# Putting the second dense layer of seven token tiles into the steps of a recurrence

## The chip, the cores and the metric

The kernel runs on one core of a Trainium2 chip. The metric is the device time of one execution in microseconds (us), the median of several runs. PE is TensorE, DVE VectorE, ACT ScalarE, POOL GpSimd and SP SyncE, which issues most of the DMAs.

## What is computed

Two branches over one sequence of 2048 tokens of width 512, mixed by a gate per token:

```python
g = _sigmoid((x * gate_w).sum(-1, keepdims=True))
a = _A_ref(x, A_mem0, A_Wq, A_Wk, A_Wv, A_Wo, A_seg_len)
b = _B_ref(x, B_w1, B_b1, B_w2, B_b2)
return g * a + (1 - g) * b
```

Branch B is an MLP: layer norm, a first dense layer from 512 to 1376 with a gelu, and a second one back to 512.

Branch A is a recurrence over 64 segments of 32 tokens. In each, 8 memory rows are put ahead of the segment's 32 tokens; the 40 rows go through attention with 32 heads of 128 and an output projection; and the first 8 rows of the result are the next segment's memory:

```python
for s in range(n_seg):
    h = jnp.concatenate([mem, xs], axis=1)
    q = jnp.einsum('btd,dhe->bhte', h, Wq)
    ...
    o = jnp.einsum('bhte,hed->btd', o, Wo)
    mem = o[:, :M, :].copy()
    outs.append(o[:, M:, :])
```

## The kernel before

All is written for one core in an order that the author fixes by hand (`manual_schedule`): each engine takes its instructions in the order in which the program emits them, and the framework only adds the waits. Line numbers are those of the kernel before, as the profile has them.

**The MLP comes first.** Tokens stand in 16 tiles of 128; a block is two tiles, so there are eight blocks (0 to 7). A block has 11 chunks of 128 hidden columns. A unit is one chunk of one block: `a_mm` (L458) computes the first layer of both tiles in four matmuls of 256 columns (L462) into one of two PSUM banks, SbF and W in turn, and ACT's gelu (L463) writes the chunk to `hTm`, of which there are two for blocks in turn. Two units later `b_mm` (L465) adds the chunk's part of the second layer, one matmul of 512 columns per tile (L468), in a bank per tile (`bp`, U[0] to U[3]). After the last chunk `ct_out` (L480) multiplies by 1 - g and stores the tile to a DRAM buffer, `c_dr`. In chunk 0 DVE takes the gates of the block before (`gates`, L449, after a tanh on ACT) and prepares the next block's layer norm (`prep`, L416); at chunks 6 and 7 (7 and 8 in block 0) PE transposes its two tiles (`prep_tr`, L437) and DVE then sums the gates (`gate_sums`, L444). The constants for the mask (L391 to L394) are made on DVE at chunk 9. At chunk 8 `loads` (L341) issues input tiles and the recurrence's weights on SP. Block 7 has the first projections of the recurrence beside it (`first`, L498: 24 units of four matmuls).

**The recurrence has 64 steps**, four (si = 0 to 3) to a token tile T. Memory rows and 24 of the tokens form the 32 columns `hT`; the eight tokens left over of each segment are gathered for a whole tile and projected as side work. PE multiplies in groups of four matmuls that use 32 columns each, side by side (`tile_position`). A step does, in PE's order: queries and keys in four banks, U[0] to U[3] (L122), each cast by ACT (L127) and transposed by DVE (L131); scores (L259, L263) in two halves, in SbF and W, on a mask that DVE has put there (`mask_put`, L250); values in X1 and X2 (L141), with ACT's casts (L719); sums over the memory queries (`msum`, L704: L270 and L273) in U[0] and U[1]; DVE's normalisation (`mnorm`, L707); sums for the token queries (`xsums`, L612: L616); the product with the values in all four U (`av`, L276: L283 and L288); the output projection of the memory rows in W (`wo_pass`, L645: L153); and the transposition that brings the new memory back into `hT` (`new_mem`, L653: L659, DVE's copy L661). After `av` ACT copies the memory part of the four U banks (L746) and then the token part (`x_raw`, L619: L622, four copies, U[3] last); `recip_x` (L625) sends the token part's reciprocals through DRAM back to all partitions (`Rb`), and POOL multiplies in the next step (`x_norm`, L638).

**Side work** is a generator (`side`, L590) that gives one group of PE work at a time; `run(n)` takes n of them at fixed places, W1 before `xsums`, W2 before `wo_pass`, W3 after it, one after each of the first two `new_mem`, and the rest at the end:

```python
WS = ((2, 3, 0), (2, 2, 2), (2, 2, 2), (2, 2, 2))
```

At si = 0 and 1 it is the next tile's left-over queries (X1) and keys (X2), at si = 3 its values (X1, X2), at si = 2 the output projection of the left-over tokens of the tile before (X1). The last tile has none at si = 0 and 1. At si = 0 the output of tile T - 2 is put together (`out_sel`, L221); it reads `c_dr` back (`c_load`, L203).

Of the kernel before, what the change touches and what calls it, by code (L numbers as in the profile page):

```python
# [27 lines left out]
def kernel(ctx, tc, A_x, A_mem0, A_Wq, A_Wk, A_Wv, A_Wo, A_seg_len, B_x, B_w1, B_b1, B_w2, B_b2, gate_w, out):  # L28
# [34 lines left out]
    g_all = pers.tile([P, NT], FP32)  # L63
    c_dr = dram.tile([S, Dm], BF16, name="c_dr")
    r_dr = [dram.tile([P, NG], FP32, name=f"r_dr{i}") for i in range(2)]
# [20 lines left out]
    make_identity(nc, ident[:])  # L86
    nc.gpsimd.memset(b1r[:], 0.0)
# [23 lines left out]
    Sb = [bk[:, 0:4 * EW].rearrange("p (i c) -> p i c", c=EW) for bk in (SbF, W)]  # L111
# [109 lines left out]
    def out_sel(T, bk):  # L221
        for si in range(SPT):
            nc.tensor.matmul(bk[32 * si:32 * si + 32, :], lhsT=SelR[:], rhs=ws.pop(SPT * T + si)[:], start=True, stop=False,
                             skip_group_check=True, tile_position=(0, 32 * si))
        wl = wls.pop(T)
        for si in range(SPT):
            nc.tensor.matmul(bk[32 * si:32 * si + 32, :], lhsT=SelL[:, 32 * si:32 * si + 32], rhs=wl[:], start=False, stop=True,
                             skip_group_check=True, tile_position=(0, 32 * si))

        def ev():  # L230
            o = cw.tile([P, Dm], BF16, tag="o", name="o")
# [15 lines left out]
    RP = [bk[:, 288:320] for bk in (SbF, W)]  # L247


    def mask_put(i2):  # L250
        c = 4 * EW + (NG + 2 * M if i2 == 0 else 0)
        nc.vector.tensor_copy(out=(SbF, W)[i2][:, 0:c], in_=MkF[:, 0:c])
# [41 lines left out]
    with tc.tile_pool(name="mlpw", bufs=1) as mlpw, \  # L294
# [7 lines left out]
        w2_sb = mlpw.tile([P, FC, Dm], BF16)  # L302
# [36 lines left out]
        m0 = ep.tile([M, Dm], BF16)  # L339
# [58 lines left out]
        for i in range(2):  # L398
            nc.gpsimd.memset(hTm[i][FR:FR + 1, FC - 1, :], 1.0)
        z_all = mlpw.tile([P, NT], FP32)  # L400
        omg = mlpw.tile([P, NT], FP32)
# [63 lines left out]
        def b_mm(blk, fc):  # L465
            rows = min(P, F - fc * P + 1)
            for tt in range(TB):
                nc.tensor.matmul(bp(blk, tt)[:], lhsT=hTm[blk % 2][:rows, fc, tt * P:(tt + 1) * P],  # L468
                                 rhs=w2_sb[:rows, fc, :], start=(fc == 0), stop=(fc == FC - 1))
            if fc == FC - 1:  # L470
                if blk < NBLK - 1:
                    ct_out(blk, 0)
                    late.append(lambda: ct_out(blk, 1))
                else:
                    for tt in range(TB):
                        ct_out(blk, tt)

# [39 lines left out]
        for n, (blk, fc) in enumerate(units):  # L517
# [15 lines left out]
            if blk + 1 < NBLK:  # L533
                f0 = 7 if blk == 0 else 6
# [10 lines left out]
            elif fc >= 1:  # L545
                if fc == 1:
                    side0 = first()
# [6 lines left out]
        for n in range(len(units) - LAG, len(units)):  # L554
            b_mm(*units[n])
        for _ in side0:
# [33 lines left out]
    def side(T, si):  # L590
# [14 lines left out]

    XRs, Rbs = {}, {}
# [38 lines left out]
    def wo_pass(U_, cuts=(0, Dm)):  # L645
        for n in range(NW):
            wo_group(W, U_, n)
        w = cw.tile([P, Dm], BF16, tag="w", bufs=8, name="w")
        for a, b in zip(cuts, cuts[1:]):
            nc.scalar.copy(out=w[:, a:b], in_=W[:, a:b])  # L650
# [14 lines left out]
    for s in range(nseg):  # L665
# [38 lines left out]
        def msum(i2):  # L704
            sums(U[i2][:, 320:352].rearrange("p (i q) -> p i q", q=8), E[:, 4 * i2:4 * i2 + 4, :], 40, 48, 8, True)

        def mnorm(i2):  # L707
            r, e = RP[i2], E[:, 4 * i2:4 * i2 + 4, 40:56].rearrange("p i (a q) -> p i a q", q=8)
            nc.vector.reciprocal(out=r, in_=U[i2][:, 320:352])
# [23 lines left out]
        if not last:  # L733
            msum(1)
# [6 lines left out]
        run(W1)  # L741
        xsums(E, 1)
# [7 lines left out]
        w = wo_pass(UT[s % 2], (0, P, 2 * P, Dm))  # L750
# [62 lines left out]
    o = cw.tile([P, Dm], BF16, tag="o", name="o")  # L813
# [128 lines left out]
```

## Time and profile before

| | |
|---|---|
| time, median of 3 runs | 770.31 us (770.07 to 771.1) |
| span of the profiled execution | 768.4 us |
| around that span, in the runs' median | 1.9 us |
| first matmul of the recurrence | 96.06 us after the span's start |

The span runs from the first to the last instruction of one execution that the profiler recorded; the profile gives no other time for it, so the runs' median is set beside it. A timeline row gives start and length in us, engine, line and operation, out<-in with partitions x elements, the count of equal instructions merged, and in brackets the engine's idle time before and what ended it.

### The profile page before, as it was taken

The numbers are of one execution on the slowest core, as the hardware profiler recorded it, in microseconds if no ns is written. First come the engines' busy times: TensorE is split into PE (matmuls) and PEld (weight loads), VectorE is DVE, ScalarE is ACT, GpSimd is POOL, SyncE is SP. The second block draws the span as 40 slices with busy tenths as digits, with TensorE's granted clock in tenths as the row PEclk, the third lists the DMA queues.
The fourth block names the chain that finished last, engine by engine and source line by source line (L and its number), as shares of the span: only waits on it lengthen the run. The fifth ranks groups of instructions, "written<-read, shape, count | busy, mean of one in ns | idle before, by whom it ended". The sixth has DMA issues, their size and how long they took to land.

```text
span 768.4 us, 43822 instructions
## 1 busy us (share of the span) xinstructions
PE 753.4 (98%) x19186; PEld 412.2 (54%) x19186; DVE 396.1 (52%) x1428; ACT 540.0 (70%) x1631; POOL 278.2 (36%) x522
## 2 busy tenths in 40 slices
PE   7999999999999999999999999999999999999996
PEld 5666554555555555555555555555555555555553
DVE  5776355445445454545554554545454555444444
ACT  4666676777777777777777777777777777777763
POOL 4111033433344443334434334443424443343341
PEclk9999999999999999999999999999999999999999
DMA  6779422223222222212131322122222213122221
GB/s 196 274 233 400 153 58 63 76 63 87 65 59 66 79 72 73 80 53 74 58 89 62 90 63 79 45 80 73 80 72 59 76 49 89 62 83 64 72 67 38
DMA packets 53319, 70.58 MB, mean 92 GB/s; under 512 B 21306, under 2 KB 43043, under 8 KB 51587
## 3 DMA queue, kind: packets, MB, share of 16 engines
q1 hardware_dynamic: 51394, 64.84, 26.8%
q8 instruction: 152, 2.49, 1.4%
q0 software_dynamic: 784, 1.97, 0.8%
q10 hardware_dynamic: 944, 0.92, 0.3%
q14 instruction: 45, 0.36, 0.2%
HBM read 56.96 MB, written 4.45 MB: 80 GB/s over the span
## 4 chain that ended last, share of the span: by engine, by line
PE 96%; DMA 1%; DVE 1%; ACT 1%; issue 0%; SPq 0%; POOL 0%; DVEq 0%; ACTq 0%
PE U L122 30%; PE X L141 18%; PE W L153 15%; PE X L122 7%; PE U L468 4%; PE U L283 4%; PE X L153 4%; PE W L462 2%; PE SbF L462 2%; PE U L270 1%; PE W L259 1%; DMA w_sb<-in_B_w_dram 1%; PE U L659 1%; PE SbF L259 1%; PE SbF L616 1%; PE U L288 1%
## 5 line engine op out<-in xcount | busy, mean ns | idle before, releaser
L643 POOL TENSOR_TENSOR UT<-XR,Rb 128x384 bf16<-128x384 bf16 x126 | 140.3, 1136 | 301.7 <-DMA Rb<-r_dr 220.5
L127 ACT CAST Tb<-U 128x512 bf16<-128x512 f32 x258 | 151.2, 586 | 78.4 <-PE U L122 78.1
L122 PEld LDWEIGHTS <-hT 128*32 128x32 bf16 x4096 | 104.5, 96 | 103.9 <-DVE hT L661 8.6
L141 PE MATMUL X<-Wv_sb,hT 128*32 128x512 bf16 x2048 | 143.8, 378 | 0.0
L122 PE MATMUL U<-Wq_sb,hT 128*32 128x512 bf16 x2048 | 136.1, 381 | 0.3 <-DVE hT L661 0.2
L122 PE MATMUL U<-Wk_sb,hT 128*32 128x512 bf16 x2048 | 132.7, 379 | 0.0
L153 PE MATMUL W<-Wo_sb,UT 128*32 128x512 bf16 x2080 | 124.6, 380 | 1.2 <-POOL racc L635 1.2
L661 DVE CAST hT<-U 128x8 bf16<-128x8 f32 x126 | 20.9, 167 | 172.8 <-PE U L659 163.6
L719 ACT CAST V<-X 128x256 bf16<-128x256 f32 x256 | 88.7, 372 | 14.5 <-PE X L141 0.8
L131 DVE STREAM_TRANSPOSE QT<-Tb 128x256 f32<-128x256 f32 x128 | 57.0, 446 | 76.5 <-ACT Tb L127 76.5
L153 PEld LDWEIGHTS <-UT 128*32 128x32 bf16 x2080 | 57.8, 96 | 56.5 <-issue 13.1
L650 ACT CAST w<-W 128x128 bf16<-128x128 f32 (+1 forms) x192 | 46.0, 311 | 48.2 <-PE W L153 48.2
L622 ACT CAST XR<-U 128x256 bf16<-128x256 f32 x252 | 78.4, 434 | 0.0
L131 DVE STREAM_TRANSPOSE KT<-Tb 128x256 f32<-128x256 f32 x128 | 57.0, 445 | 28.0 <-ACT Tb L127 23.5
L643 POOL TENSOR_TENSOR UL<-XR,Rb 128x128 bf16<-128x128 bf16 x126 | 60.3, 502 | 0.0
L141 PEld LDWEIGHTS <-hT 128*32 128x32 bf16 x2048 | 46.4, 94 | 21.0
L635 POOL TENSOR_TENSOR racc<-racc,R 128x72 f32<-128x72 f32 x63 | 21.3, 338 | 93.4 <-PE U L288 84.1
L468 PE MATMUL U<-w_sb,hTm 128*128 128x512 bf16 (+1 forms) x176 | 52.4, 381 | 0.0
L746 ACT CAST UT<-U 128x64 bf16<-128x64 f32 x252 | 35.4, 226 | 22.9 <-PE U L288 22.8
L462 PEld LDWEIGHTS <-w_sb 128*128 128x128 bf16 (+1 forms) x352 | 34.5, 102 | 20.1 <-issue 1.3
L702 ACT ACTIVATE E<-W 128x64 bf16<-128x64 f32 (+1 forms) x128 | 35.0, 273 | 11.3 <-PE W L263 11.3
L659 PEld LDWEIGHTS <-w 128*32 128x32 bf16 x1008 | 22.8, 93 | 37.2 <-ACT w L650 29.3
(159 smaller groups left out, 1204.7 us busy)
## 6 DMA issues: line engine op xcount, KB each, us to landing
Rb<-r_dr SPq DMA_DIRECT2D x63, 512.0 KB, 3.8
Wv_sb<-in_A_Wv_dram SPq DMA_DIRECT2D x4, 1024.0 KB, 6.3
Wq_sb<-in_A_Wq_dram SPq DMA_DIRECT2D x4, 1024.0 KB, 7.1
Wk_sb<-in_A_Wk_dram SPq DMA_DIRECT2D x4, 1024.0 KB, 9.4
Wo_sb<-in_A_Wo_dram SPq DMA_DIRECT2D x4, 1024.0 KB, 15.0
VP<-VL SPq DMA_DIRECT2D x64, 64.0 KB, 3.5
c<-c_dr SPq DMA_DIRECT2D x16, 128.0 KB, 3.6
xt<-in_A_x_dram SPq DMA_DIRECT2D x15, 128.0 KB, 3.1
```

Of the source, the lines that this page charges most:

```text
L122: nc.tensor.matmul(bk[32 * j:32 * j + 32, :], lhsT=G[:, kc, :], rhs=W5[t][:, kc, h0:h1, j, :], start=(kc == 0), stop=(kc == KC - 1), tile_ ...
L127: nc.scalar.copy(out=Tb[:], in_=bk.rearrange("p (a b e) -> p a e b", a=8, b=2))
L131: nc.vector.transpose(out=dst[:, 8 * hf:8 * hf + 8, c0:c0 + 32, :].rearrange("p a r b -> p a (r b)").bitcast(FP32), in_=Tb[:].rearrange("p ...
L141: nc.tensor.matmul(bk[32 * j:32 * j + 32, :], lhsT=G[:, kc, :], rhs=Wv5[:, kc, 4 * vb:4 * vb + 4, j, :], start=(kc == 0), stop=(kc == KC - ...
L153: nc.tensor.matmul(bk[32 * c:32 * c + 32, :], lhsT=U_[:, j, i, :], rhs=Wo_sb[:, 4 * i + j, :], start=(n == 0), stop=(n == NW - 1), tile_po ...
L462: nc.tensor.matmul(hp[:rows, 0:TB * P], lhsT=w1_sb[:, kc, fc * P:fc * P + rows], rhs=yTs[blk][:, kc, :], start=(kc == 0), stop=(kc == KC - 1))
L468: nc.tensor.matmul(bp(blk, tt)[:], lhsT=hTm[blk % 2][:rows, fc, tt * P:(tt + 1) * P], rhs=w2_sb[:rows, fc, :], start=(fc == 0), stop=(fc = ...
L622: nc.scalar.copy(out=XR[:, j], in_=U[j][:, 0:NG * 40].rearrange("p (i q) -> p i q", q=40)[:, :, 0:32])
L643: nc.gpsimd.tensor_tensor(out=out[:, :, 4 * h:4 * h + 4, o:o + b - a], in0=XR[:, :, 4 * h:4 * h + 4, a:b], in1=Rb[:, h, :, :, a:b], op=ALU ...
L650: nc.scalar.copy(out=w[:, a:b], in_=W[:, a:b])
L719: nc.scalar.copy(out=V[:, i0:i0 + 2, :].rearrange("p i e -> p (i e)"), in_=(X1, X2)[vb][:, 256 * h:256 * h + 256])
L746: nc.scalar.copy(out=UT[s % 2][:, j, :, 0:M], in_=U[j][:, 0:NG * 40].rearrange("p (i q) -> p i q", q=40)[:, :, 32:40])
```

## The change

Seven tiles (3, 5, 7, 11, 13, 14, 15) get only the first layer in the MLP. Their activations are stored to DRAM (`spill`) and loaded back chunk by chunk in the recurrence, where the second layer is done in half groups: four matmuls of 32 columns and 256 output columns side by side, two half groups to a chunk. They are taken from a generator, one ahead of `msum(1)` and one after `run(W1)` in each step, and as side work of the last tile at si = 0 and 1. They add up in bank W until a tile's 11 chunks are through, and DVE then scales and stores it. W's other uses move: the second half of the scores to U[0], `wo_pass` to X2, `msum` to U[1] and U[3], the first two `new_mem` to U[0] and U[1], the second stream of the left-over projections from X2 to U[3], and the reciprocals RP[1] to SBUF. In blocks whose second tile is put off, the transposes for the next block are emitted at chunks 8 and 9. Output tiles have one buffer in place of two.

```diff
+    DEF = (3, 5, 7, 11, 13, 14, 15)
+    h_dr = {T: dram.tile([FC, P, P], BF16, name=f"h_dr{T}") for T in DEF}
...
-    Sb = [bk[:, 0:4 * EW].rearrange("p (i c) -> p i c", c=EW) for bk in (SbF, W)]
+    Sb = [bk[:, 0:4 * EW].rearrange("p (i c) -> p i c", c=EW) for bk in (SbF, U[0])]
...
-    RP = [bk[:, 288:320] for bk in (SbF, W)]
+    RS = ep.tile([P, 32], FP32)
+    RP = [SbF[:, 288:320], RS[:]]
...
-            for tt in range(TB):
+            tts = [tt for tt in range(TB) if blk * TB + tt not in DEF]
+            for tt in tts:
                 nc.tensor.matmul(bp(blk, tt)[:], lhsT=hTm[blk % 2][:rows, fc, tt * P:(tt + 1) * P],
...
+        def spill(blk, a, b):
+            for tt in range(TB):
+                T = blk * TB + tt
+                if T in DEF:
+                    src = hTm[blk % 2][:, :, tt * P:(tt + 1) * P]
+                    nc.sync.dma_start(h_dr[T][a:b].rearrange("f p t -> p f t"), src[:, a:b])
...
-                f0 = 7 if blk == 0 else 6
+                f0 = 8 if (blk + 1) * TB - 1 in DEF else 7 if blk == 0 else 6
+                if fc == 2 and blk >= 1:
+                    spill(blk - 1, 0, FC)
...
+                if fc == 2:
+                    spill(blk - 1, 0, FC)
+                if fc == 7:
+                    spill(blk, 0, 6)
...
+        spill(NBLK - 1, 6, FC)
...
-            gens = [[left_qk(T + 1, 0, 0, X1), left_qk(T + 1, 1, 0, X2)], [left_qk(T + 1, 0, 1, X1), left_qk(T + 1, 1, 1, X2)], [],
-                    [left_v(T + 1, 0, X1), left_v(T + 1, 1, X2)]][si]
+            gens = [[left_qk(T + 1, 0, 0, X1), left_qk(T + 1, 1, 0, U[3])], [left_qk(T + 1, 0, 1, X1), left_qk(T + 1, 1, 1, U[3])], [],
+                    [left_v(T + 1, 0, X1), left_v(T + 1, 1, U[3])]][si]
+        elif si < 2:
+            gens = [mlp_units(8)]
...
+    def hm_load(n):
+        for _ in range(n):
+            if work:
+                T, fc = work.pop(0)
+                hm = cw.tile([P, P], BF16, tag="hm", bufs=5, name="hm")
+                nc.sync.dma_start(hm[:], h_dr[T][fc])
+                hms.append((T, fc, hm))
+
+    def mlp_out(T):
+        ct = cw.tile([P, Dm], BF16, tag="o", bufs=1, name="ct")
+        nc.vector.tensor_scalar(out=ct[:], in0=W[:], scalar1=omg[:, T:T + 1], scalar2=None, op0=ALU.mult)
+        nc.sync.dma_start(c_dr[T * P:(T + 1) * P, :], ct[:])
+
+    def mlp_halves():
+        hm_load(4)
+        while hms:
+            T, fc, hm = hms.pop(0)
+            for h in range(2):
+                cc = slice(256 * h, 256 * h + 256)
+                for c in range(4):
+                    nc.tensor.matmul(W[32 * c:32 * c + 32, cc], lhsT=hm[:, 32 * c:32 * c + 32], rhs=w2_sb[:, fc, cc],
+                                     start=(fc == 0 and h == 0), stop=(fc == FC - 1), skip_group_check=True, tile_position=(0, 32 * c))
+                if h == 1:
+                    hm_load(1)
+                    if fc == FC - 1:
+                        mlp_out(T)
+                yield
+
+    def mlp_units(n):
+        for _ in range(n):
+            next(mlp, None)
+            next(mlp, None)
+            yield
...
-        bk = (U[1][:, 0:M], U[3][:, 0:M], xs8z)[n]
+        bk = (U[0][:, 0:M], U[1][:, 0:M], xs8z)[n]
...
-            sums(U[i2][:, 320:352].rearrange("p (i q) -> p i q", q=8), E[:, 4 * i2:4 * i2 + 4, :], 40, 48, 8, True)
+            sums(U[1 + 2 * i2][:, 320:352].rearrange("p (i q) -> p i q", q=8), E[:, 4 * i2:4 * i2 + 4, :], 40, 48, 8, True)
...
         if not last:
+            next(mlp, None)
             msum(1)
             mnorm(1)
...
         run(W1)
+        next(mlp, None)
         xsums(E, 1)
...
-        w = wo_pass(UT[s % 2], (0, P, 2 * P, Dm))
+        w = wo_pass(UT[s % 2], (0, P, 2 * P, Dm), X2)
```

More of the change, by code (lines that the diff above doesn't have):

```diff
@@ L470, in b_mm @@
             if fc == FC - 1:
[L471 to L475, printed above, removed]
-                        ct_out(blk, tt)
+                for tt in tts:
+                    if tt == 0 or blk == NBLK - 1:
+                        ct_out(blk, tt)
+                    else:
+                        late.append(lambda: ct_out(blk, 1))
+        def spill(blk, a, b):
[4 more added lines that the diff above has]
+                    nc.sync.dma_start(h_dr[T][a:b].rearrange("f p t -> p f t"), src[:, a:b])
         late = []
@@ L604, in extra @@
         return iter(())
+    work = [(T, fc) for T in DEF for fc in range(FC)]
+    hms = []
+    def hm_load(n):
[28 more added lines that the diff above has]
+            yield
+    mlp = mlp_halves()
     XRs, Rbs = {}, {}
```

23 lines of the change are left out of this document (12 added, 11 removed).

## The prediction

> **What bounds the kernel now.** I read the cores view first, then parts 1 and 4 of the page.
>
> ```profile
> core 0: 768.4 us, clock 0.996
> PE 753.4 (98%) x19186; PEld 412.2 (54%) x19186; DVE 396.1 (52%) x1428; ACT 540.0 (70%) x1631; POOL 278.2 (36%) x522
> PE 96%; DMA 1%; DVE 1%; ACT 1%; issue 0%; SPq 0%; POOL 0%; DVEq 0%; ACTq 0%
> ```
>
> The reader is to see that the chain that ended last is PE's for 96% of the span. Matmul rows include a pipelined tail, so "busy" doesn't say whether PE has room; starts do. Next, the timeline of one MLP block (PE, then DVE), and of block 7 (PE, then ACT).
>
> ```profile
> 28.88 0.60 PE L462 MATMUL SbF<-yT,w_sb 128*128 128x256 bf16 x4
> 29.32 0.59 PE L468 MATMUL U<-w_sb,hTm 128*128 128x512 bf16 x2
> 29.75 0.60 PE L462 MATMUL W<-yT,w_sb 128*128 128x256 bf16 x4
> ...
> 34.98 0.40 PE L441 MATMUL X<-ident,y 128*128 128x128 bf16 x4
> 35.21 0.60 PE L462 MATMUL W<-yT,w_sb 128*128 128x256 bf16 x4
> ```
> ```profile
> 30.18 0.17 DVE L452 TENSOR_SCALAR g_all<-th 128x2 f32<-128x2 f32 x1 [1.31 <-ACT th L451]
> ...
> 34.51 0.73 DVE L434 TENSOR_SCALAR y<-xt,mv,rs 128x512 bf16<-128x512 bf16 x2
> ...
> 36.51 0.42 DVE L442 COPY yT<-X 128x512 bf16<-128x512 bf16 x1 [0.67 <-PE X L441]
> ...
> 38.67 0.23 DVE L394 TENSOR_SCALAR MkF<-MkF,mk 128x8 bf16<-128x8 bf16 x1
> ```
> ```profile
> 84.03 0.60 PE L462 MATMUL SbF<-yT,w_sb 128*128 128x256 bf16 x4
> ```
> ```profile
> 84.72 0.47 ACT L463 ACTIVATE hTm<-SbF,b_sb 128x256 bf16<-128x256 f32 x1
> ```
>
> One unit there is 0.44 us for L462 plus 0.43 us for two L468, with no gap: PE bounds the MLP, at 0.217 us per second-layer matmul. Four transposes take 35.21 - 34.98 = 0.23. Then a step of the recurrence (24, first of its tile, si = 0) on PE, DVE and ACT.
>
> ```profile
> 344.19 1.11 PE L122 MATMUL U<-Wq_sb,hT 128*32 128x512 bf16 x16
> ...
> 349.57 0.61 PE L141 MATMUL X<-Wv_sb,hT 128*32 128x512 bf16 x8
> 350.08 0.20 PE L270 MATMUL U<-E,BO 128*32 128x32 bf16 x4
> ...
> 350.77 0.22 PE L616 MATMUL SbF<-BO,E 128*32 128x4 bf16 x8
> 350.93 0.30 PE L283 MATMUL U<-E,V 32*128 32x40 bf16 x16
> ...
> 351.21 0.29 PE L283 MATMUL U<-E,V 32*128 32x40 bf16 x16
> ...
> 351.91 0.39 PE L122 MATMUL X<-Wk_sb,GL 128*32 128x512 bf16 x4
> 352.12 1.90 PE L153 MATMUL W<-Wo_sb,UT 128*32 128x512 bf16 x32
> ```
> ```profile
> 350.93 0.22 DVE L710 TENSOR_TENSOR E<-E,W 128x64 bf16<-128x64 bf16 x1
> ```
> ```profile
> 351.57 0.56 ACT L746 CAST UT<-U 128x64 bf16<-128x64 f32 x4 [0.35 <-PE U L288]
> 351.99 1.25 ACT L622 CAST XR<-U 128x256 bf16<-128x256 f32 x4
> ```
>
> A group of four 32-column matmuls runs side by side: 351.91 to 352.12 is 0.216 us for 512 columns, so a half group of 256 takes 0.108. Last, from the chain of waits, two starts of an ordinary si = 1 step, and from the timeline the same step of the last tile, which has no side work.
>
> ```profile
> 355.32 3.45 PE U L122 x63
> 365.46 3.55 PE U L122 x64
> ```
> ```profile
> 728.07 1.05 PE L122 MATMUL U<-Wq_sb,hT 128*32 128x512 bf16 x16
> ...
> 735.41 1.91 PE L153 MATMUL W<-Wo_sb,UT 128*32 128x512 bf16 x32 [0.39 <-POOL racc L635]
> ...
> 738.22 0.62 PE L122 MATMUL U<-Wq_sb,hT 128*32 128x512 bf16 x8
> ```
>
> With eight side units (8 x 0.216 = 1.73 us) the step takes 365.46 - 355.32 = 10.14 us, without them 738.22 - 728.07 = 10.15. So a step is a chain through all engines, side work lies in its gaps, and what delays a link of the chain is paid in full.
>
> **The change part by part.** *Removed.* Seven tiles x 11 chunks = 77 matmuls of L468, 77 x 0.217 = **16.7 us** of PE in the MLP, of which not all comes out:
> - DVE is late next. From the gates (30.18) it needs 5.06 us to both y (35.24), some 4.7 to the first. Then follow on PE that tile's transposes (0.23), one unit with one tile put off (0.44 + 0.22) and the second transposes (0.23), so the second yT copy starts no sooner than some 6.1 us after the gates (4.7 + 1.1, and an estimated 0.2 from PE's last start to DVE's). From that copy to the end of the mask constants DVE needs 38.90 - 36.51 = 2.4. The next gates thus come no sooner than 8.5 us after the last, where PE would be through in 11 x 0.65 + 2 x 0.23 = 7.6. Blocks 1 to 3 hand this on; followed through to block 5's start I lose 2.9 us. Without mask constants, block 6 loses 0.5.
> - Block 7 loses both tiles. Its first-layer units alternate between two banks, and a bank comes free 84.72 + 0.47 - 84.03 = 1.16 us after its matmuls start: 0.58 a unit, not 0.44. Gate tanhs that wait for DVE's sums stand in the same ACT queue. The 24 side units spare half of this; I take 1.0.
>
> That leaves 16.7 - 2.9 - 0.5 - 1.0 = **12.3 us gained** (bounds 9 and 16.7). ACT's and POOL's share of the result copies and stores goes too, off the chain.
>
> *Spills.* A tile's activations leave in 11 x 128 rows of 256 bytes, on SP behind 2 MB of weights. A buffer's gelu two blocks on waits until the spill has read it.
>
> ```profile
> Wq_sb<-in_A_Wq_dram SPq DMA_DIRECT2D x4, 1024.0 KB, 7.1
> VP<-VL SPq DMA_DIRECT2D x64, 64.0 KB, 3.5
> r_dr<-R SPq DMA_DIRECT2D x63, 4.0 KB, 1.5
> ```
> ```profile
> 96.73 1.17 SPq L487 DMA_DIRECT2D c_dr<-ct  x2
> ```
>
> Weights land 7.1 us after issue, a spill behind them some 2 later, and the buffer is wanted about 8.6 us after that issue: 0 to 1.3 us late, for three blocks. I take **1.0 us** (0 to 4).
>
> *First load.* The first activations come back only after the last spills have landed, since their buffers lie where the MLP's lay. From the recurrence's start: last gelu 0.7 us, two issues 1.17, landing 1.5 to 3.5 (r_dr and VP), the load 0.5 to issue and 1.5 to 3.5 to land: 5.4 to 9.4 us. The first half group stands ahead of L270, 350.08 - 344.19 = 5.9 us into a step. I take **1.5 us** once (0 to 4). What waits behind that load on PE is msum(1) and the whole chain.
>
> The Trainium skill ("DMA: Bandwidth & Descriptors", Specifications) says that transfers under 512 B are read, modified and written. No row here shows the spill; r_dr's 32-byte rows landing in 1.5 us against 3.5 for VP's 512-byte rows don't show such a penalty. If the rule doubled the spills' time, the third rival would be the likelier.
>
> *Half groups.* 124 of 154 come two to a step, 0.108 us each. The first fills PE's wait for the exponentials: V's two groups end at 349.57 + 0.43 = 350.00 and L270 starts at 350.08. The second delays L616 and the first L283, but the second L283 (351.21) waits for DVE's E (350.93 + 0.22 = 351.15), and between 350.77 and 351.21 PE has about 0.1 us to give. I take 0.01 us a step, **0.6 us** (0 to 13.4, all of 124 x 0.108 if the gaps weren't there). The seven 512-wide DVE copies, once in eleven steps, stand ahead of the x part's reciprocals; the next step's Wo is the first to need those, and POOL's product is the cover. Cost 0.
>
> *Bank moves.* Scores' second half in U[0], sums in U[1] and U[3], Wo in X2, new memory in U[0] and U[1]: each is read by something that its next writer awaits anyway (U[0]'s next writer needs hT from the same DVE copy). Cost 0; that chain is the cover. One move has none. At si = 0, W2 = 3 puts the first K unit of the next tile between x_raw and wo_pass. It went to X2, free since the V copies; it goes to **U[3]**, which x_raw copies last. In the built program its first matmul waits for ACT's count after the fourth L622. PE works in order: Wo's eight groups, the memory rows and the next step are queued behind it. The same pair of rows in the first and in the last of the 15 steps that have it (T = 0 to 14):
>
> ```profile
> 103.39 0.39 PE L122 MATMUL X<-Wk_sb,GL 128*32 128x512 bf16 x4
> ```
> ```profile
> 103.47 1.24 ACT L622 CAST XR<-U 128x256 bf16<-128x256 f32 x4
> ```
> ```profile
> 683.78 0.39 PE L122 MATMUL X<-Wk_sb,GL 128*32 128x512 bf16 x4
> ```
> ```profile
> 683.86 1.24 ACT L622 CAST XR<-U 128x256 bf16<-128x256 f32 x4
> ```
>
> The unit started at 103.39 and U[3] is free at 104.71; 683.78 and 685.10; at step 24, 351.91 and 353.24: 1.32 us each, plus about 0.05 for the release. 15 x 1.37 = **20.5 us lost** (18 to 21.5). At si = 1 and 3 the U[3] units stand after Wo, when the copies are over: 0.
>
> *Last tile.* Steps 60 and 61 take up to eight whole chunks each as side work, from five buffers with four chunks loaded ahead. In step 60 the sixth chunk (65) is the last unit ahead of Wo.
>
> ```profile
> 723.46 0.40 PE L141 MATMUL X<-Wv_sb,hT 128*32 128x512 bf16 x4
> ...
> 725.26 1.91 PE L153 MATMUL W<-Wo_sb,UT 128*32 128x512 bf16 x32 [0.39 <-POOL racc L635]
> ```
>
> Its buffer comes free with chunk 60, about 723.8 on these rows, and it is wanted at about 725.4; issue and landing take 2.0 to 4.0, so Wo starts 0.4 to 2.7 us late. I take **1.8 us**. Step 61 finds its chunks loaded.
>
> Of these terms only the first can be a gain: each of the others adds work or a wait, and takes none off the chain. **Sum:** -12.3 + 1.0 + 1.5 + 0.6 + 20.5 + 1.8 = +13.1 us. The span goes from 768.4 to 781.5; the runs' median, 770.31, is 1.9 above the span, and I keep that: **783.4 us**.
>
> **The rivals.**
> 1. *The U[3] wait is absorbed, and the kernel is faster.* If a si = 0 step had slack behind Wo, the late start would vanish; from 13.1 / 15 = 0.87 us of slack a step on, the sign turns. For it: without side work steps don't shorten, so PE has room. Against: that room lies ahead of Wo and in the wait for ACT's w copies, which follow Wo. Fully absorbed: 783.4 - 20.5 = 762.9. Chance 7%.
> 2. *The half groups cost what they take.* The gaps are of the order of the half group; if a release comes late behind it, all 13.4 us are paid, 12.8 over my term: 796. For it: 0.08 us before L270 is under 0.108. Against: the second gap. Chance 8%.
> 3. *Small packets clog the queue.* Seven spills of 1408 packets among saturated weights; if each takes much longer than a weight's share, the first load and the gelus come late by 10 us more: 793. Chance 12%.
>
> That the work isn't moved can be left out: the built program has 99 L468 matmuls and 616 half-width ones.
>
> **How the numbers follow.** My case has 73%; its own bounds give 776 to 790. The clogged queue's smaller half is taken in: range 776 to 791. A measurement of this kernel tells about 0.2% (1.5 us). Faster: rival 1 and my bounds' tail, 0.08. Within: 0.01. Slower: 0.91.
>
> **What would show it.** L468's count at 99 and the recurrence's first U<-Wq,hT at about 85 us, not 96.06; in si = 0 steps a PE wait of some 1.3 us for ACT's XR ahead of Wo, steps of about 12.0 us; other steps within 0.05 us of 10.15 to 10.23; one wait for the load in step 0 and one in step 60. I am wrong if the si = 0 steps stay at 10.6, if the others grow by 0.1 or more, or if the recurrence starts after 90.

## The result, and the profile after

| | before | after |
|---|---|---|
| time, median of 4 runs each on the same chip | 770.7 us (770.07 to 772.6) | 809.87 us (806.16 to 812.2) |
| span of the profiled execution | 768.4 us | 807.0 us |

The changed kernel is slower, by a ratio of 1.050 (95% interval 1.0478 to 1.0522). The direction was forecast; the size, 13.1 us, was a third of the 38.7 us that the spans show.

First the cores view of the changed kernel, and from its page the line of PE and the chain that ended last.

```profile
core 0: 807.0 us, clock 0.988
```
```profile
PE 752.3 (93%) x19716; PEld 422.7 (52%) x19725; DVE 406.7 (50%) x1433; ACT 537.2 (67%) x1626; POOL 275.7 (34%) x518
```
```profile
PE 79%; ACT 3%; DMA 3%; issue 1%; DVE 1%; POOL 1%; SPq 0%; DVEq 0%; POOLq 0%
```

PE is as many microseconds busy as before (752.3 against 753.4) in a span that is 38.7 us longer: the new time is waiting, not work. (The chain's 79% can't be set against the 96% of before: this chain is followed back only to 100.2 us after the span's start, so its shares add up to 88.) The step starts (first U<-Wq,hT of each step) tell where. The column is after minus before, in us:

| part of the span | after minus before |
|---|---|
| up to the recurrence's start (94.80, was 96.06) | -1.26 |
| step 0 (15.05, was 10.58) | +4.48 |
| the other 14 steps with si = 0 and T below 15 | +19.55 |
| the 45 steps with si = 1 to 3 and T below 15 | +6.21 |
| steps 60 to 62, the last tile | +10.65 |
| last step and end | -0.95 |
| span | +38.68 |

**In the MLP** the 77 matmuls are gone, and nearly all of the gain with them. The timeline of ACT, then of PE, at the two places:

```profile
41.09 0.47 ACT L467 ACTIVATE hTm<-W,b_sb 128x256 bf16<-128x256 f32 x1 [4.16 <-DMA h_dr<-hTm]
```
```profile
65.05 0.47 ACT L467 ACTIVATE hTm<-W,b_sb 128x256 bf16<-128x256 f32 x1 [4.54 <-DMA h_dr<-hTm]
```
```profile
41.62 0.60 PE L466 MATMUL W<-yT,w_sb 128*128 128x256 bf16 x4 [3.69 <-ACT hTm L467]
```
```profile
65.57 0.60 PE L466 MATMUL W<-yT,w_sb 128*128 128x256 bf16 x4 [3.47 <-ACT hTm L467]
```

A gelu stands still until the spill has read its buffer, and PE behind it. Then the windows (PE, PEld, DVE, ACT and POOL busy, and after them the granted clock, the DMA engines' share and GB/s), with the first of them in the kernel before at the end:

```profile
40.00:45.00 5.00, 3.12 (x17) 2.10 (x18) 2.96 (x14) 2.82 (x7) 0.54 (x1) 0.80 0.95 350
45.00:50.00 5.00, 5.00 (x39) 3.56 (x38) 2.67 (x10) 2.62 (x6) 0.00 (x0) 0.86 0.61 179
...
65.00:70.00 5.00, 4.43 (x22) 2.69 (x22) 3.84 (x19) 3.87 (x9) 1.08 (x2) 0.68 1.02 401
```
```profile
40.00:45.00 5.00, 5.00 (x36) 3.23 (x34) 4.28 (x20) 3.66 (x10) 1.08 (x2) 1.00 0.90 354
```

Behind each stall the granted clock is 0.68 to 0.86, where it is 1.00 in the same windows of before: what PE does after the wait takes longer too. The Trainium skill ("TensorE: Matmul & The Clock Gate", Part 1) says that PE falls to half clock after an idle window of some 3.4 us; stalls of 3.69 and 3.47 us with a lowered clock behind them agree. The length of a stall alone doesn't tell, though. In e3 (below) PE stands still for 3.55 us up to 41.19, and the clock stays at 1.00:

```profile
40.00:45.00 5.00, 3.77 (x29) 2.75 (x29) 3.33 (x16) 3.60 (x9) 0.54 (x1) 1.00 0.95 337
```

PE's first unit starts later as well. PE before and after, then POOL before and after:

```profile
7.74 0.16 PE L512 MATMUL W<-ident,b1r 11*128 11x11 bf16 x1 [0.61 <-DMA b1r<-in_B_b_dram]
```
```profile
9.10 0.16 PE L523 MATMUL W<-ident,b1r 11*128 11x11 bf16 x1 [1.91 <-POOL SelL L381]
```
```profile
1.52 0.70 POOL L88 DMA_DIRECT2D b1r<-in_B_b_dram  x1
```
```profile
1.01 0.53 POOL L91 MEMSET w_sb<- 32x512 bf16 x1
...
2.35 0.70 POOL L93 DMA_DIRECT2D b1r<-in_B_b_dram  x1 [0.16 <-POOL BO L95]
```

The bias is loaded on POOL behind a new memset of w2's last rows; the load is issued at 2.35, not at 1.52, and the transposition of the bias, for which PE's first unit waits, comes 1.36 us later. (The row names POOL's SelL, which ended last. The second of the two bias loads landed at 8.96, 1.36 us after the 7.60 of before; 0.83 of that is the issue, the rest a slower landing.)

**At si = 0** the wait is the one foreseen. From the waits (us in total, times, longest), and from the timeline of step 24 (ACT, then PE):

```profile
PE U L127 <- ACT XR L680: 16.4, 15, 1.2
```
```profile
364.90 1.24 ACT L680 CAST XR<-U 128x256 bf16<-128x256 f32 x4
```
```profile
366.19 0.40 PE L127 MATMUL U<-Wk_sb,GL 128*32 128x512 bf16 x4 [1.21 <-ACT XR L680]
366.41 1.91 PE L158 MATMUL X<-Wo_sb,UT 128*32 128x512 bf16 x32
```

15 waits, each in front of Wo; these steps' median is 12.02 us, 1.38 over the 10.64 of before.

**In step 0** (PE, then POOL):

```profile
100.18 0.28 PE L265 MATMUL SbF<-QT,KT 128*32 128x40 bf16 x16 [1.75 <-DVE KT L136]
...
104.61 0.22 PE L289 MATMUL U<-E,V 32*128 32x40 bf16 x6 [0.99 <-issue]
```
```profile
98.36 1.42 POOL L591 MEMSET UT<- 128x768 bf16 x2 [12.34 <-ACT Tb L132]
```

The scores are late, before any half group is reached: DVE's QT and POOL's UT are first written at about 98.4, though PE's queries had been running since 94.80. POOL's row names ACT's cast, which ended at 98.25. But the first cast, which is all that QT's first transposition needs (before, it starts 0.1 us behind it), had ended at 97.18. What ended just before QT is the last spill, which landed 2.5 us after its issue, at 98.14; e5 below shows the same wait alone. The first half group itself starts at 102.10 without a wait: its load landed at about 100.9.

```profile
95.62 0.53 SPq L487 DMA_DIRECT2D h_dr<-hTm  x1
```

The 0.99 us inside the product with the values (L289) have no releaser in the profile, and their cause stays open.

**In the last tile** PE waits for chunks (PE, SP, and the window behind the longest wait):

```profile
755.31 0.40 PE L649 MATMUL W<-w_sb,hm 128*32 128x256 bf16 x8 [0.92 <-DMA hm<-h_dr]
...
760.28 0.40 PE L649 MATMUL W<-w_sb,hm 128*32 128x256 bf16 x8 [2.04 <-DMA hm<-h_dr]
...
774.41 0.62 PE L649 MATMUL W<-w_sb,hm 128*32 128x256 bf16 x8 [3.30 <-DMA hm<-h_dr]
```
```profile
767.72 0.42 SPq L688 DMA_DIRECT2D r_dr<-R  x1
770.84 0.32 SPq L689 DMA_DIRECT2D Rb<-r_dr  x1
771.25 0.39 SPq L634 DMA_DIRECT2D hm<-h_dr  x1
```
```profile
775.00:780.00 5.00, 4.57 (x60) 1.69 (x48) 2.45 (x7) 1.17 (x2) 2.42 (x4) 0.50 0.14 43
```

The last load stands on SP behind the storing and reading back of the reciprocals, is issued at 771.25 and wanted three microseconds before it lands; the clock behind it is 0.50.

### The profile page after: what moved, and what is told of

The parts are those of the page before. It is cut to its first block, busy times and chain, and to the rows that moved or that the text cites. A ratio compares the mean times of both kernels' runs of the same rounds, so it can differ in the third digit from the quotient of the medians.

```text
span 807.0 us, 44966 instructions
## 1 busy us (share of the span) xinstructions
PE 752.3 (93%) x19716; PEld 422.7 (52%) x19725; DVE 406.7 (50%) x1433; ACT 537.2 (67%) x1626; POOL 275.7 (34%) x518
## 4 chain that ended last, share of the span: by engine, by line
PE 79%; ACT 3%; DMA 3%; issue 1%; DVE 1%; POOL 1%; SPq 0%; DVEq 0%; POOLq 0%
PE U L127 31%; PE X L158 16%; PE X L146 15%; PE U L289 3%; PE X L127 3%; ACT XR L680 2%; PE W L649 2%; PE U L146 2%; PE U L265 1%; DMA r_dr<-R 1%; ACT UT L806 1%; PE U L717 1%; DMA hm<-h_dr 1%; PE SbF L265 1%; PE SbF L674 1%
## 5 line engine op out<-in xcount | busy, mean ns | idle before, releaser
L132 ACT CAST Tb<-U 128x512 bf16<-128x512 f32 x288 | 168.8, 587 | 89.3 <-PE U L127 84.6
L158 PE MATMUL X<-Wo_sb,UT 128*32 128x512 bf16 x2016 | 121.2, 380 | 1.2 <-POOL UT L701 0.7
L708 ACT CAST w<-X 128x128 bf16<-128x128 f32 x189 | 44.7, 309 | 69.6 <-PE X L158 69.6
L127 PE MATMUL U<-Wk_sb,GL 128*32 128x512 bf16 x496 | 38.7, 378 | 16.4 <-ACT XR L680 16.4
L649 PE MATMUL W<-w_sb,hm 128*32 128x256 bf16 x616 | 41.3, 274 | 6.7 <-DMA hm<-h_dr 6.7
L127 PEld LDWEIGHTS <-GL 128*32 128x32 bf16 x1024 | 26.1, 94 | 33.8 <-issue 23.2
```

What stands on the lines that cost most here:

```text
L127: nc.tensor.matmul(bk[32 * j:32 * j + 32, :], lhsT=G[:, kc, :], rhs=W5[t][:, kc, h0:h1, j, :], start=(kc == 0), stop=(kc == KC - 1), tile_ ...
L132: nc.scalar.copy(out=Tb[:], in_=bk.rearrange("p (a b e) -> p a e b", a=8, b=2))
L158: nc.tensor.matmul(bk[32 * c:32 * c + 32, :], lhsT=U_[:, j, i, :], rhs=Wo_sb[:, 4 * i + j, :], start=(n == 0), stop=(n == NW - 1), tile_po ...
L649: nc.tensor.matmul(W[32 * c:32 * c + 32, cc], lhsT=hm[:, 32 * c:32 * c + 32], rhs=w2_sb[:, fc, cc], start=(fc == 0 and h == 0), stop=(fc = ...
L708: nc.scalar.copy(out=w[:, a:b], in_=bk[:, a:b])
```

## The experiments

Theory A is the prediction's frame, a sum of local waits: the unit in U[3], and what the trace after showed besides, the spills, the last tile, step 0. Theory B, its rival, is that the half groups or their loads slow the steps throughout. Each kernel's trace gives the parts of its span, in us against before's (start of the recurrence; step 0; the other 14 steps with si = 0; the 45 with si = 1 to 3; steps 60 to 62). The ratios are to the kernel before, run on the same chip.

| run | median | ratio (95%) | start | step 0 | si = 0 | si 1-3 | 60-62 |
|---|---|---|---|---|---|---|---|
| after | 809.87 | 1.050 (1.0478-1.0522) | -1.3 | +4.5 | +19.6 | +6.2 | +10.7 |
| e1 moves only | 792.2 | 1.0273 (1.0256-1.0291) | +1.0 | +1.4 | +19.0 | +1.2 | +0.4 |
| e2 moves, late unit | 769.5 | 0.9983 (0.9973-0.9992) | +0.3 | -0.2 | -2.0 | +0.4 | +0.3 |
| e3 after, late unit | 787.66 | 1.0212 (1.0194-1.0231) | -1.4 | +2.5 | -0.7 | +5.1 | +13.2 |
| e4 spills from ACT | 807.8 | 1.0459 (1.0426-1.0492) | -0.5 | +3.4 | +20.5 | +4.7 | +12.4 |
| e5 e3, three buffers | 779.98 | 1.0119 (1.0102-1.0136) | -10.9 | +7.1 | -0.9 | +6.9 | +11.8 |
| e6 e3, five tiles | 780.99 | 1.0137 (1.012-1.0154) | +3.5 | +1.4 | +1.8 | +4.1 | +0.2 |
| e7 e6, three buffers, memset | 770.15 | 0.9992 (0.9978-1.0007) | -7.9 | +1.2 | +2.3 | +6.5 | +0.2 |
| e8 e7, four loads | 768.12 | 0.997 (0.9956-0.9985) | -8.9 | +1.3 | +2.2 | +3.6 | +0.0 |
| e9 before, late unit | 768.84 | 0.998 (0.9969-0.9991) | +0.0 | -0.2 | +0.0 | +0.2 | -0.0 |
| e10 e3, weights behind spills | 778.64 | 1.0108 (1.0086-1.013) | -10.1 | +3.2 | -0.4 | +3.3 | +11.8 |
| e11 two tiles, first place | 770.53 | 0.9995 (0.9978-1.0012) | -2.8 | +1.9 | -0.0 | +5.2 | +0.1 |
| e12 two tiles, second place | 769.9 | 0.9996 (0.9983-1.0008) | -3.0 | +0.2 | -1.7 | +3.3 | +0.0 |
| e13 all repairs, five tiles | 768.89 | 0.9963 (0.9949-0.9977) | -8.5 | +1.4 | +1.1 | +4.8 | +0.2 |
| e14 e10, loads from ACT | 774.64 | 1.0041 (1.0018-1.0064) | -10.7 | +3.2 | +0.2 | +7.5 | +7.1 |

The columns are of one profiled execution each; executions of one kernel lie up to 5.3 us to either side of their median, most within 3, so a difference of 2 us in the columns of many steps proves nothing, and the first, second and last are the sure ones.

**e1: the bank moves without the deferred tiles.**

```diff
-    DEF = (3, 5, 7, 11, 13, 14, 15)
+    DEF = ()
```

> The changed kernel with no tile put off (DEF is empty): only the bank moves are left, no spills, no loads, no half groups. Theory A (the moves cost only the wait on U[3] at si = 0): 15 steps of about 12.02 us in place of 10.64, all other steps as before, 770.5 + 20 = about 790.5 us. Theory B (moving scores, sums, Wo and new memory among the banks costs something in every step): the other steps grow too, 795 us or more.

792.2 us, and the waits of e1 have the row of the changed kernel again:

```profile
PE U L127 <- ACT XR L680: 17.1, 15, 1.2
```

The 15 steps take 20.4 us more (1.4 + 19.0), the others about as before. The U[3] unit alone costs 20 us, and neither spills nor half groups have part in it.

**e2: the moves, with the unit behind Wo.**

```diff
-    WS = ((2, 3, 0), (2, 2, 2), (2, 2, 2), (2, 2, 2))
+    WS = ((2, 2, 1), (2, 2, 2), (2, 2, 2), (2, 2, 2))
```

> As the run with the bank moves alone, but at si = 0 the third side unit, the first on U[3], is taken after wo_pass (WS (2, 2, 1) in place of (2, 3, 0)). Theory A: the wait on U[3] is gone and nothing else was lost, 770.5 us within 1.5. Theory B: still 4 us or more over the kernel before.

769.5 us: the wait is gone without one in its place, and the other bank moves cost nothing.

**e3: the changed kernel with that one edit.**

> The changed kernel with all seven tiles put off, and at si = 0 the third side unit after wo_pass. Theory A: the si = 0 steps go from 12.02 to about 10.7, 809.9 - 19.5 = about 790.5 us. Rival (PE is so full with half groups that the unit costs the same elsewhere): under 12 us better, 798 or more.

787.66 us, 22.2 less than the changed kernel, where 19.5 were expected; the spans of the two profiled executions differ by 21.0. So 17 us over before remain that have nothing to do with U[3]: 13.2 in the last tile, 5.1 in the steps with si = 1 to 3, 2.5 in step 0, and an MLP that gains 1.4 where 11.3 were expected.

**e4: the spills issued by ACT.** In the changed kernel:

```diff
-                    nc.sync.dma_start(h_dr[T][a:b].rearrange("f p t -> p f t"), src[:, a:b])
+                    nc.scalar.dma_start(h_dr[T][a:b].rearrange("f p t -> p f t"), src[:, a:b])
```

> The changed kernel with the spills issued by ACT in place of SP. Theory A (the spills land late because they stand on SP's queue behind 2 to 4 MB of weights): a spill lands within some 4 us, the two waits of gelu for h_dr<-hTm (8.7 us) and the half clock after them go, the recurrence starts at about 86 us, 809.9 - 8 = about 802 us. Rival (rows of 256 bytes to DRAM are slow in themselves, or the DMA engines are simply full): landing stays near 10 us, within 2 us of 809.9.

My theory that they wait in SP's queue, behind the weights there, was wrong in this form: 807.8 us, 2 less, where 8 were expected. The spill of tile 3 in e4, from its DMA issues (KB, us to landing), and the waits of the gelus:

```profile
h_dr<-hTm ACTq DMA_DIRECT2D x1, 352.0 KB, 10.1
```
```profile
ACT hTm L467 <- DMA h_dr<-hTm: 7.7, 2, 3.9
```

From a queue of its own this spill, issued 0.6 us behind two of the weights on SP, lands 10.1 us after issue (9.9 from SP), and the gelus still wait. The Trainium skill ("DMA: Bandwidth & Descriptors", Issuing engines are not separate DMA queues) says that transfers run on the same 16 DMA engines whichever engine issues them; this run agrees.

**e5: a third activation buffer** (and two MLP result buffers in place of four), on e3.

```diff
-        hTm = [mlpw.tile([P, FC, TB * P], BF16, name=f"hTm{i}") for i in range(2)]
+        hTm = [mlpw.tile([P, FC, TB * P], BF16, name=f"hTm{i}") for i in range(3)]
```

> The run with the late third unit (787.7 us), with three hTm buffers in place of two, so that a buffer is wanted again one block (about 8 us) later; room for it comes from the result buffers ct, 2 in place of 4. Theory A (a spill lands 9.7 us after its issue, some 4 us after the gelu that writes its buffer again is due): the waits of gelu for h_dr<-hTm go, the half clock behind them too, and the recurrence starts at 86 to 87 us, 787.7 - 8 = about 780 us. Rival (DMA traffic, not the buffer, holds the MLP): under 3 us better.

779.98 us, as expected. The recurrence starts at 85.20, 9.4 us sooner than in e3: the gelus' wait was worth that, with the clock behind it. But step 0 grows to 17.65. PE, then POOL:

```profile
93.81 0.33 PE L265 MATMUL SbF<-QT,KT 128*32 128x40 bf16 x16 [4.97 <-DMA hm<-h_dr]
```
```profile
91.98 1.42 POOL L591 MEMSET UT<- 128x768 bf16 x2 [15.56 <-DMA h_dr<-hTm]
```

The releaser of POOL's row is the spill: the recurrence's tiles lie where the activations lay, and can't be written until the last spills have read them. QT's first transposition follows the landing of the last spill (91.76) by 0.3 us here, and by 0.3 in the changed kernel, so that is the wait of its step 0 too, where the late MLP hid most of it. Of 9.4 us won 4.6 are given back.

**e6: five tiles** (3, 5, 7, 11, 13), on e3.

> The run with the late third unit, with five tiles put off (3, 5, 7, 11, 13): 55 chunks, all done by step 54, so the last tile's steps have no chunks, and the MLP's last block is as before. Theory A (the last tile's loads stand behind SP's waits for r_dr and Rb, and PE's idle there halves its clock): steps 60 to 62 go from 14.1, 16.3 and 13.3 us to about 10.2 each, 13 us less; step 0 loses its wait for the last spills, 2 us less; the MLP's last block takes 5 to 6 us more: 787.7 - 9 = about 778 us. Rival (the last tile's steps are long because PE has no room for the chunks): the same or worse than 787.7.

780.99 us, 3 more than expected. Steps 60 to 62 take 30.7 us in place of 43.7. The chunks taken in the last tile thus cost 13 us there; the MLP is 4.9 us longer, since the second layer of two tiles is back in it.

**e7: the five tiles, with three buffers, and the memset behind the b1 loads.**

```diff
-    nc.gpsimd.memset(w2_sb[FR:P, FC - 1, :], 0.0)
     nc.gpsimd.memset(b1r[:], 0.0)
 ...
+    nc.gpsimd.memset(w2_sb[FR:P, FC - 1, :], 0.0)
     nc.gpsimd.memset(BO[:], 0.0)
```

> Late third unit, five tiles, three hTm buffers (ct 2), and the memset of w2's last rows behind the loads of b1 on POOL. Theory A: the MLP waits go (8 us) and 1 to 2 us at the start: 778 - 9 = about 769 us, near the bank moves alone (769.5) and the kernel before (770.7); what the MLP saves, some 8 us, is about what step 0 and longer waits in the steps cost. Rival (half groups lie in gaps, nothing else is lost): 762 us.

PE's first unit starts at 8.12 (9.20 in the changed kernel), the recurrence at 88.13. All 7.9 us won there are spent again: 1.2 in step 0, 9.1 in the steps behind it up to 62.

**e8: the same, but only the first four chunks are loaded.**

```diff
-                hm = cw.tile([P, P], BF16, tag="hm", bufs=5, name="hm")
-                nc.sync.dma_start(hm[:], h_dr[T][fc])
-                hms.append((T, fc, hm))
+                if len(hmk) < 4:
+                    hm = cw.tile([P, P], BF16, tag="hm", bufs=5, name="hm")
+                    nc.sync.dma_start(hm[:], h_dr[T][fc])
+                    hmk.append(hm)
+                hms.append((T, fc, hmk[min(fc % 4, len(hmk) - 1)]))
```

> The run with five tiles and these mends, but only the first four chunks are loaded back; all 110 half groups multiply those (so the second layer of the five tiles is not the reference's). It leaves out 51 loads of 32 KB. Theory A (the extra waits of 0.2 to 1.2 us inside runs of equal PE instructions come from PE's instruction fetch, which the loads' traffic delays): some 4 to 6 us less than with the loads. Theory B (they come from the 16 instructions more per step, or the half groups themselves): within 1 us.

768.12 against 770.15: the 51 loads left out are worth some 2.0 us, though the two intervals still overlap. The other steps are still 5.8 us longer than before's (2.2 + 3.6), so neither of the two expectations holds alone: most stays without the loads.

**e9: the kernel before, with the late unit.**

> The kernel before with one edit: at si = 0 the third side unit stands after the output projection instead of before it (WS[0] = (2, 2, 1)). Tells what the 1.2 us that the bank moves with the later unit gained over before (769.5 against 770.7) came from. Theory: the later unit alone, which lets wo_pass start 0.1 us sooner in 15 steps: si = 0 steps 10.53 instead of 10.64, 769.0 to 769.7 us. Rival: the bank moves (Wo in X2, scores in U[0]) gain it: si = 0 steps stay at 10.64, 770.3 to 771 us.

768.84, ratio 0.998. That is e2's gain without e2's moves, so the medians speak for the late unit. The trace does not show it: in the profiled execution si = 0 steps are 10.60 at the median, where 10.53 was expected, and no part but step 0 is shorter, that by 0.2. The gain stands, its place is not shown.

**e10: the weights issued right behind the spills.** On e3, blocks 1 to 6 issue their weights at chunk 3 in place of 8:

```diff
                 if fc == 2 and blk >= 1:
                     spill(blk - 1, 0, FC)
 ...
+                if fc == (3 if blk >= 1 else 8):
+                    weights(blk)
                 if fc == 8:
                     loads(blk)
```

> The changed kernel with the unit after Wo (787.7 us, start of the recurrence at 94.6), and in blocks 1 to 6 the recurrence's weights are issued at chunk 3, right behind the spill of the block before, instead of at chunk 8, ahead of the next spill. Theory: the spills are late because their packets wait for the weights issued ahead of them. Then they land in 2 to 4 us instead of 9.9, the gelus' waits of 8 us and the half clock behind them go, and the recurrence starts at 85 to 88; step 0 may then wait up to 5 us for the last spills, which still stand where they stood: 779 to 784 us. Rival: a spill of 1408 rows takes its 8 to 10 us whatever lies ahead of it: waits, start (94 to 95) and time (787 to 788) stay.

The same spill, of tile 3, first in the changed kernel, then here: SP's rows, and its issue with KB and us to landing.

```profile
29.81 0.90 SPq L319 DMA_DIRECT2D Wv_sb<-in_A_Wv_dram  x2
30.82 0.38 SPq L487 DMA_DIRECT2D h_dr<-hTm  x1
```
```profile
h_dr<-hTm SPq DMA_DIRECT2D x1, 352.0 KB, 9.9
```
```profile
31.13 0.38 SPq L488 DMA_DIRECT2D h_dr<-hTm  x1
31.56 1.59 SPq L319 DMA_DIRECT2D Wq_sb<-in_A_Wq_dram  x2
```
```profile
h_dr<-hTm SPq DMA_DIRECT2D x1, 352.0 KB, 3.8
```

And the windows in which it is issued, with the DMA engines' share and GB/s last, in the changed kernel and here:

```profile
30.00:31.00 1.00, 0.90 (x7) 0.49 (x5) 0.96 (x6) 0.74 (x3) 0.00 (x0) 1.00 0.89 205
```
```profile
30.00:31.00 1.00, 1.00 (x9) 0.76 (x8) 1.00 (x5) 0.77 (x3) 0.00 (x0) 1.00 0.03 7
```

778.64 us, just under the theory's 779 to 784. Behind 2 MB of weights the spill lands after 9.9 us, ahead of them after 3.8. No gelu waits for a spill any more, and the clock stays up:

```profile
40.00:45.00 5.00, 4.75 (x40) 3.45 (x38) 4.31 (x19) 3.65 (x8) 0.54 (x1) 1.00 0.95 275
...
65.00:70.00 5.00, 4.80 (x39) 3.38 (x38) 4.38 (x16) 3.75 (x9) 1.39 (x4) 1.00 0.78 206
```

The start comes at 86.01, 8.6 us sooner than e3's, with two buffers and with the same transfers. With e4 this settles the spills: it is not the rows' size and not the issuing queue, it is the weights already in flight. A spill that still stands behind weights in e10, tile 13's at 74.83 behind Wo's, again lands only after 9.9.

**e11 and e12: one half group a step, at one place.** Two tiles (5 and 11), late unit, three buffers, memset moved; e11 keeps the half group ahead of msum(1), e12 the one ahead of the token sums.

```diff
-        run(W1)
-        next(mlp, None)
+        run(W1)
```

> Two tiles put off (5 and 11), one half group a step, only ahead of msum(1) (44 in steps 0 to 43); the unit after Wo, three activation buffers, and the memset behind the b1 loads. Read from the steps that carry a half group (1 to 43) against those of the same si behind them (45 to 59). Theory of the prediction: the place is a gap, the steps grow by 0.00 to 0.02 us each, and about 767 us come out (3 us gained in the MLP, 1.2 by the late unit). Rival 1: any further PE work costs about half its time, 0.05 to 0.06 a step: 769 to 770. Rival 2: this place costs all of 0.108 a step, and the other nothing: 771 to 772.

> As the run before it, but the one half group a step stands after run(W1), ahead of the token sums, instead of ahead of msum(1). Theory of the prediction: 0.01 us a step, about 767 us, the same as with the other place. Rival 1: 0.05 to 0.06 a step at either place, 769 to 770. Rival 2: this place alone costs, up to 0.108 a step, 771 to 772, while the first is free.

770.53 and 769.9: with intervals this wide, no difference between the places. At si = 1 and 3 the medians of steps 1 to 43 are within 0.01 us of before's (10.16 and 10.23), so there neither place costs a fixed amount per step. At si = 2 they are 10.25 and 10.34, against 10.23: that the second place costs its 0.1 in these eleven steps can't be ruled out from one execution. Both kernels take some 3 us more than the 767 of the theory, as much as the first rival said, but not spread over all steps as the rival had it. Step 0 tells the places apart: 1.9 and 0.2 over before, since the first load is wanted later at the second. The other columns of the two can't be compared, since the profiled execution was e11's slowest and e12's fastest.

**e13: all repairs together.** Five tiles, late unit, weights behind the spills, memset behind the b1 loads.

> All that the runs so far point to, together: five tiles put off (3, 5, 7, 11, 13), the unit after Wo, the weights issued behind the spills, the memset behind the b1 loads. Sum of what they measured: 778.6 for the seven tiles with the weights behind the spills, less 11.8 in the last tile (its three steps 42.4 against 30.6), plus about 3 for two tiles' second layer back in the MLP (start at 88 to 89), less 1.5 for the memset, less 1 to 2 for a shorter wait in step 0: 766 to 767 us, faster than the kernel before with the late unit alone (768.8). Rival: what the half groups add in scattered places (3 to 6 us over the steps with two of them) takes it back: 769 to 771.

768.89, ratio 0.9963: 0.4% under before, and not to be told from e9. It lies between the two expectations; the rival's scattered cost (4.8 us at si = 1 to 3) took some of the gain. In the rows:

```profile
94.56 0.29 PE L652 MATMUL W<-w_sb,hm 128*32 128x256 bf16 x4 [1.44 <-DMA hm<-h_dr]
```

The first load is as late as the prediction said (1.5), but not for its reason: tiles 14 and 15 have no spill here, and the last one was issued at 72.12. What stands ahead of the load on SP is the result of the last block, for which SP waits 8.4 us until DVE has made it:

```profile
88.24 1.01 SPq L499 DMA_DIRECT2D c_dr<-ct  x2
...
92.12 2.95 SPq L637 DMA_DIRECT2D hm<-h_dr  x5
```

**e14: the last 13 chunks loaded from ACT's queue**, on e10.

```diff
-                nc.sync.dma_start(hm[:], h_dr[T][fc])
+                (nc.scalar if T * FC + fc >= 14 * FC + 9 else nc.sync).dma_start(hm[:], h_dr[T][fc])
```

> The seven tiles with the unit after Wo and the weights behind the spills (778.6 us), and the last 13 chunks, those loaded from step 60 on, are loaded from ACT's queue instead of SP's. Theory: in the last tile the chunks come late because their loads stand on SP behind the reciprocals' store and its reading back, which wait for DVE, and behind the output's copies. Then steps 60 to 62 fall from 42.4 towards 33 to 36 us: 769 to 772. Rival: a chunk's own way of 3 us from issue to landing with five buffers sets the pace (a chunk every 0.6 us at least): steps 60 to 62 stay at 40 to 43, 777 to 779, or ACT's issues delay its casts and they grow.

774.64 us. Steps 60 to 62 fall from 42.4 to 37.7, between the two expectations. The place in SP's queue was thus some 4.7 of the 11.8 us lost there (4.0 by the medians, and this kernel's runs lie between 770.62 and 779.91). Of the rest the rows show two waits:

```profile
740.26 0.40 PE L652 MATMUL W<-w_sb,hm 128*32 128x256 bf16 x8 [1.75 <-DMA hm<-h_dr]
```
```profile
728.57 1.82 ACTq L637 DMA_DIRECT2D hm<-h_dr  x3
731.27 0.58 ACT L132 CAST Tb<-U 128x512 bf16<-128x512 f32 x1 [2.48 <-DMA hm<-h_dr]
```

A chunk is still late by its own way and the five buffers, and ACT's cast of the next step's queries now comes behind ACT's own load issues. Part of the wait moved with the queue.

## Why the prediction was wrong

| term | predicted | measured |
|---|---|---|
| MLP, with the spills | -12.3 + 1.0 | -1.3 |
| step 0, without its U[3] wait | +1.5 | +3.1 |
| U[3] wait, 15 steps | +20.5 | +20.4 (e1) |
| half groups | +0.6 | 5 to 6 |
| last tile | +1.8 | +10.7 |

Of the prediction's own signs of being wrong, one came clearly: the recurrence starts after 90, at 94.80.

- **The U[3] wait: right**, in mechanism, place, count and size. Rival 1, that it is absorbed, is refuted by e1: a delay ahead of Wo is paid in full.
- **The MLP's gain: right, but it never came out.** When the spills no longer stop the gelus, the start is 10.1 us earlier (e10), and the memset moved adds some 1.0 (first unit at 8.19 in e13, 9.20 in the changed kernel): 11.1 of the 12.3, as a sum of two runs, for none has both with seven tiles.
- **Spills: the step that failed first.** The term said that a spill lands "some 2 later" than the weights ahead of it, and so costs 1.0 us, 4 at most. Counted from the weights' issue (29.81), it had the spill landed after 7.1 + 2 = 9.1 us and the buffer wanted after 8.6. The spill of tile 3 landed at 40.7, after 10.9 us. The buffer was wanted at an estimated 37.1, after 7.3: the gelu's matmuls start at 36.44, and in block 7's rows a gelu follows its matmuls' start by 0.7. So it was some 3.5 us late in place of 0.5, and tile 7's was no better (4.54 us of waiting).

```profile
36.44 0.61 PE L466 MATMUL W<-yT,w_sb 128*128 128x256 bf16 x4
```

Two blocks lost 3.5 to 3.7 us of PE each, and the lowered clock behind them was not in the term at all. Against e3, whose two stalls are 3.55 and 4.25 us, e10 puts the whole at 8.6, over twice the upper bound.
- **The memset** of w2's last rows was not in the sum. An instruction in front of a load issue on POOL's queue delayed that issue by 0.83 us, and PE's first unit came 1.37 us later.
- **Step 0: about twice the size, and another cause.** The prediction had it that the load comes back only after the last spills, since their buffers lie where the MLP's lay; it did not see that the same holds for QT, KT and UT, which the scores need earlier. e5 shows it undisguised. In the changed kernel the load itself is not waited for. That e13's first load is 1.44 us late, for a predicted 1.5, is luck, since no spill stands ahead of it there.
- **Last tile: the term that was mis-sized by most**, with the spills. "Step 61 finds its chunks loaded" was false. The term counted one late buffer; it left out that the later loads are queued on SP behind transfers that wait for other engines (e14: some 4.7 us of it), and that the clock falls behind the longest wait (3.30 us, then 0.50). Its range of 0.4 to 2.7 comes out as 0.4 to 2.4 from its own figures, which changes nothing.
- **Half groups: right for the typical step, wrong in the sum.** That the first one fills a gap is shown: before has the row below for steps 1 to 59 (PEld, waiting for nothing that the profile names), and the changed kernel has none for that line.

```profile
PEld L270 <- issue: 13.9, 59, 0.3
```

The medians of si = 1 to 3 are 10.16, 10.23 and 10.24, against 10.16, 10.23 and 10.23. Rival 2, all 13.4 us paid, is refuted. But in the eleven kernels with half groups and all their loads these 45 steps are 3.3 to 7.5 us longer in sum, and in the three without 0.2 to 1.2. The added time sits in single steps. One can be read: step 11 takes 11.49, and its chain runs through the copy of tile 3's result on DVE and late reciprocals (start, us, what):

```profile
212.24 0.10 DVE ct L639
...
213.46 3.66 DMA r_dr<-R
...
217.17 5.21 DMA Rb<-r_dr
...
222.52 2.18 POOL UT L701 x2
```

Rb's median is 3.9 us; here 5.21, behind the copy that I had costed at nothing because POOL's product covers it. It is not a fixed price: in e10, with the same seven tiles, that step takes 10.34. Nor are the others all chance: step 46 takes 11.0 to 11.8 us in all six kernels with seven tiles, and 10.23 before. For these the cause stays open: e8 gives the loads about 2 us, and e11 and e12 show as much with 44 half groups as others with 110, which speaks against a price per half group.

- **Rival 3** came near in effect (gelus late by some 8 us) and wrong in mechanism: the same 1408 rows land in 3.8 us when no weights lie ahead.

The sum was the right frame, since it holds with the measured terms: -1.3 + 4.5 + 19.6 + 6.2 + 10.7 - 1.0 = 38.7. Two bounds in it were too narrow, those of the spills and of the last tile, both for waits on a DMA; and the memset and the memory under QT, KT and UT were not in it.

## What to carry to other kernels

A transfer that frees a buffer should be issued ahead of the bulk loads, not behind them; the queue that issues it matters little as long as the DMA engines are full of those loads. A long wait of PE on a DMA is to be costed with the lowered clock that can follow it (here behind waits of 3.3 to 3.7 us, though not behind each), and a memory that is reused holds up everything that is laid over it, not just the tile one thinks of. And before work is moved into gaps, look for the one unit whose order costs a full wait: here the order of one PE unit was worth 20 us, and the moved work, with five tiles and the found losses repaired, gained nothing that can be told from the late unit alone (ratios 0.9963 and 0.998 to before).

## What the runs showed that was not expected

- A spill of 352 KB took 9.9 us behind 2 MB of weights on the same queue, 10.1 from another queue at the same time, and 3.8 ahead of them.
- Three PE waits of 3.3 to 3.7 us in the changed kernel were each followed by a lowered clock: 0.80 and 0.86, 0.68, and 0.50 over whole windows of 5 us. In e3 a wait of 3.55 us was not, and one of 2.40 us up to 736.50 was (0.57 from 735 to 740).
- Executions of one kernel can differ by several us: e11's ran from 767.19 to 773.64. In the longest of them, the profiled one, the median steps are still within 0.05 us of before's, and the added time sits in single longer steps.
